# Pooled attention and an MLP on one core: value products as full-array matmuls plus 32-row tiles, batches prepared two groups ahead

## The chip, the core and the metric

The kernel runs on one core of a Trainium2 chip. A core has a matrix engine (TensorE, "PE" in the profile, with its weight loads listed apart as "PEld"), three engines for elementwise work (VectorE "DVE", ScalarE "ACT", GpSimd "POOL") and a queue engine (SyncE, "SP"), which here issues nearly all DMAs. Each engine executes its own instructions in the order in which the program emits them, and waits in place for what it needs from the others. Operands lie in SBUF, in 128 partitions; TensorE writes to PSUM, and another engine copies the result out.

The metric is device time in microseconds, the median over runs. A profiled execution of the same program gives the trace.

## What is computed

Inputs are `q`, `k`, `v` of shape 8 batches x 8 heads x 576 positions x 64, and two weight matrices. Keys and values are averaged over groups of 8 positions, so that each head has 72 pooled rows; attention is taken over these, and the result goes through an MLP without residual:

```python
k_p = k.reshape(B, H, Sp, 8, D).mean(axis=3)          # Sp = 72
v_p = v.reshape(B, H, Sp, 8, D).mean(axis=3)
attn = softmax(q @ k_p.transpose(0, 1, 3, 2) / sqrt(D))
x = (attn @ v_p).transpose(0, 2, 1, 3).reshape(B * S, H * D)   # 4608 x 512
out = gelu_tanh(x @ w_in) @ w_out                      # d_ff = 2048
```

## The kernel before

**Groups.** The 4608 tokens are worked in nine groups of 512. Group b holds the first 512 tokens of batch b; the remainder group R holds the last 64 tokens of all eight batches. The order is 0, 1, ..., 6, R, 7 (`seq`); `n_` is the place in that order. In a group, subtiles j = 0..3 have 128 tokens each.

**Stages of a group's attention.** Loads bring `q`, `k` and `v` as f32 (`load_q`, `load_main`, and `load_half` for the 64 pooled rows that do not fill a block). `cast_q` (L117) makes bf16, and `q_transpose_dma` (L198) transposes it by DMA. `pool` (L122) sums eight rows in three DVE additions into `kvb`; the factor 1/8 is applied later. `dup_k`, `k_transpose_dma` (L177) and `k_spread` (L181) give `kbd`, in which the two heads of a pair lie block-diagonally, so that one matmul yields the scores of both. `scores` (L202) and `exps` (L218) follow, then `norm` (L225): a row sum and a reciprocal on DVE, and one multiplication that writes `eb` in bf16, on DVE for subtiles 0, 2, 3 and on POOL for subtile 1. `e_transpose_dma` (L243) turns each subtile's `eb` into a part of `eT`, with pooled rows on the partitions.

**Value products.** 8 heads x 72 = 576 pooled rows lie end to end in five blocks of 128 (the first one holds 64 zeros). A head pair has 144 rows, and these lie in two blocks; `PARTS` names the two (block, operand) combinations of each pair. `spread_v` (L143) multiplies pooled v by the 0/0.125 mask `vmask` into eight operands of 128 x 128 per batch, `vbd`, on POOL. `values` (L259) runs two full products for each of the four pairs, 512 columns each, into two PSUM tiles `xo`; ACT copies each to `xT`. For group R each batch has its own 64 columns, so there are 64 products of 64 columns (L272). Group 0 uses `values_half` (L249) on halves of 256 columns.

**MLP and hooks.** `mlp` (L309) runs 64 matmuls of the hidden stage (L296, with Gelu on ACT) and then, for each of four row blocks r, 16 output matmuls (L301), a copy to `osb` and a store. Attention work of later groups is woven in by position: `at(hooks, s, f, ...)` puts a call ahead of the matmul number s. Positions 0 to 63 are the hidden stage, 64 + 16 r + fo the output stage. While group g's MLP runs, the next group n gets its scores at positions 67, 69, 78 and 82, its norms and eT transposes at 79, 82, 86 and 90, and its value products at 121, seven output matmuls before the next hidden stage. A position fixes only the order within each engine's queue; DVE, POOL and SP run ahead of PE as far as their waits allow. The stage called "group 2" in this document is the MLP of group 1 (`n_ == 1`), in which group 2's attention is made.

**What is loaded when.** Around position 91 of a group's MLP, k and v of the group after next are loaded (`load_kv`, L484); they are pooled at positions 12 to 41 of the next group's MLP. The q of the group after next is loaded at 57, cast on POOL and transposed at 91. Group R's own q is loaded in four portions at 92. Tiles `kvb` and `q_sb` have two buffers, the raw `kv` tile three (shared with the weights), `qT`, `kTd` and `eT` one.

**Group 0.** There is no MLP under which its attention could lie, so PE alternates short warm-up matmuls, transposes and scores with what DVE, ACT and POOL deliver (L361 to L463). Its MLP (`mlp_first`) works on token halves.

The softmax here doesn't subtract the row's maximum and nothing guards it: scores larger than these inputs give would overflow.

## Time and profile before

| | before |
|---|---|
| median of 3 runs | 301.4 us (301.17 to 301.49) |
| profiled execution | 301.36 us |
| its span | 299.3 us |
| PE busy | 290.7 us, 1734 matmuls |
| DVE / ACT / POOL busy | 146.7 / 158.2 / 55.5 us |
| value products, groups 1 to 7 (L266) | 56 matmuls, 512 columns |
| value products, group R (L272) | 64 matmuls, 64 columns |
| DMA moved | 56.3 MB, 188 GB/s on average |

The span runs from the first to the last instruction of the program; the profiled time has 2.1 us around it. A matmul's recorded length holds the passage through the array and overlaps its neighbours (379 ns for 512 columns); what it costs in a row of matmuls is the distance of the starts. The chain of waits shows these distances summed by piece. "Landing" is the time from a DMA's issue until its last byte is there. A line of the timeline merges neighbouring instructions of one kind: start, length, engine, line, operation, output and inputs, count, and in brackets the idle time ahead of it with what ended it.

### The profile page before, as it was taken

How to read it: one execution, taken by the hardware profiler on the slowest of the kernel's cores; microseconds unless marked ns; L12 is line 12 of the kernel's file. 1: busy time of each engine (PE TensorE's matmuls, PEld its weight loads, DVE VectorE, ACT ScalarE, POOL GpSimd, SP SyncE). 2: the span in 40 equal slices, each digit the busy share in tenths (PEclk: the TensorE clock that was granted, in tenths of full speed). 3: DMA queues.
4: the chain of work that ended last, by engine and by line, in shares of the span. 5: the costliest groups of instructions: out<-in, count | busy, mean ns of one | idle time of the engine just before them, and what ended most of it. 6: DMA issues, size and time to landing. Idle time of an engine off the chain costs nothing.

```text
span 299.3 us, 4581 instructions
## 1 busy us (share of the span) xinstructions
PE 290.7 (97%) x1734; PEld 151.6 (51%) x1734; DVE 146.7 (49%) x241; ACT 158.2 (53%) x242; POOL 55.5 (19%) x71
## 2 busy tenths in 40 slices
PE   7869999999999999999999999999999999999996
PEld 7748844445444544454445444544444544444444
DVE  6895769164706570648073807381639100920012
ACT  1477783667157715672477246724773267426500
POOL 3252033230400240024012400240024000100000
PEclk9999999999999999999999999999999999999999
DMA  7999997995699459947993599049944800351012
GB/s 235 357 387 338 384 350 132 343 279 158 135 279 250 145 127 271 269 146 126 261 297 134 119 249 301 4 107 249 276 147 101 164 36 2 79 114 37 0 70 70
DMA packets 73221, 56.32 MB, mean 188 GB/s; under 512 B 45808, under 2 KB 55408, under 8 KB 73200
## 3 DMA queue, kind: packets, MB, share of 16 engines
q1 hardware_dynamic: 73056, 55.98, 68.2%
q8 instruction: 13, 0.21, 0.3%
q10 hardware_dynamic: 144, 0.07, 0.1%
q14 instruction: 8, 0.07, 0.1%
HBM read 36.70 MB, written 9.44 MB: 154 GB/s over the span
## 4 chain that ended last, share of the span: by engine, by line
PE 91%; DMA 3%; DVE 2%; SPq 1%; POOL 1%; issue 0%; POOLq 0%
PE mm L296 41%; PE mm L301 41%; PE xo L266 4%; DMA q_sb<-in_q_dram 3%; PE sc L208 2%; PE mm L329 1%; POOL eb L231 1%; SPq L98 1%; PE xo L272 1%; PE tp L193 1%; PE sc L213 0%; DVE w_in_b L80 0%; PE tp L240 0%; DVE w_out_b L80 0%; POOL q_b L80 0%; PE xo L255 0%
## 5 line engine op out<-in xcount | busy, mean ns | idle before, releaser
L301 PE MATMUL mm<-w_out_b,gT 128*128 128x512 bf16 x560 | 128.6, 379 | 0.5 <-DVE w_out_b L80 0.5
L296 PE MATMUL mm<-xT,w_in_b 128*128 128x512 bf16 (+1 forms) x640 | 127.6, 358 | 0.5 <-DVE xT L80 0.5
L298 ACT ACTIVATE gT<-mm 128x512 bf16<-128x512 f32 (+1 forms) x160 | 88.4, 555 | 47.0 <-PE mm L296 45.9
L296 PEld LDWEIGHTS <-w_in_b 128*128 128x128 bf16 x640 | 62.2, 98 | 62.6 <-issue 0.5
L301 PEld LDWEIGHTS <-gT 128*128 128x128 bf16 x560 | 53.4, 98 | 59.7 <-DVE w_out_b L80 0.7
L80 DVE COPY osb<-mm 128x512 f32<-128x512 f32 (+2 forms) x37 | 24.3, 658 | 62.9 <-PE mm L301 60.8
L78 ACT CAST xT<-xo 128x1024 bf16<-128x1024 f32 (+1 forms) x18 | 16.6, 966 | 56.8 <-PE xo L266 49.1
L228 DVE TENSOR_REDUCE den<-e 128x8 f32<-128x576 f32 x36 | 26.5, 736 | 38.0 <-ACT e L221 37.9
L148 POOL TENSOR_TENSOR vbd<-kvb,vmask 128x256 bf16<-128x256 bf16 (+2 forms) x40 | 21.2, 553 | 113.5 <-DVE kvb L130 113.4
L128 DVE TENSOR_TENSOR kv<-kv 128x1024 f32<-128x1024 f32 (+3 forms) x20 | 22.4, 1118 | 29.7 <-DMA kv<-in_v_dram 27.7
L231 DVE TENSOR_TENSOR eb<-e,r 128x576 bf16<-128x576 f32 x28 | 27.2, 970 | 1.0
L221 ACT ACTIVATE e<-sc 128x576 f32<-128x576 f32 x36 | 22.5, 650 | 9.6 <-ACT e L221 4.0
L231 POOL TENSOR_TENSOR eb<-e,r 128x576 bf16<-128x576 f32 x8 | 10.1, 1266 | 71.5 <-ACT e L221 41.1
L80 POOL CAST q_b<-q_sb 128x2048 bf16<-128x2048 f32 (+1 forms) x7 | 15.0, 2147 | 4.1 <-DMA q_sb<-in_q_dram 4.1
L208 PEld LDWEIGHTS <-qT 128*128 128x128 bf16 x128 | 10.1, 98 | 7.0 <-ACT qT L78 0.6
L208 PE MATMUL sc<-kbd,qT 128*128 128x144 bf16 x128 | 13.2, 226 | 0.2 <-ACT qT L78 0.2
L266 PE MATMUL xo<-eT,vbd 128*128 128x512 bf16 x56 | 13.2, 379 | 0.0
L129 DVE TENSOR_TENSOR kv<-kv 128x512 f32<-128x512 f32 (+3 forms) x20 | 12.8, 640 | 0.7
L410 PE MATMUL warm<-identb 128*128 128x128 bf16 x112 | 9.1, 249 | 1.4 <-POOL vmask L398 1.4
L494 ACT ACT_TABLE_LOAD x8 | 10.3, 1283 | 0.1
L80 DVE COPY kbd<-kTd 64x288 bf16<-64x288 bf16 x12 | 5.6, 467 | 8.3 <-DMA kTd<-kvb 8.2
L314 ACT ACT_TABLE_LOAD x7 | 9.0, 1283 | 0.1
(55 smaller groups left out, 99.5 us busy)
## 6 DMA issues: line engine op xcount, KB each, us to landing
out_dram<-osb SPq DMA_DIRECT2D x31, 256.0 KB, 6.7
kv<-in_k_dram SPq DMA_DIRECT2D x7, 1024.0 KB, 6.5
q_sb<-in_q_dram SPq DMA_DIRECT2D x7, 1024.0 KB, 5.9
kv<-in_v_dram SPq DMA_DIRECT2D x7, 1024.0 KB, 9.9
w_in_s<-in_moe_w_in_dram SPq DMA_DIRECT2D x4, 1024.0 KB, 13.0
w_out_s<-in_moe_w_out_dram SPq DMA_DIRECT2D x4, 1024.0 KB, 13.8
out_dram<-osb SPq DMA_DIRECT2D x9, 128.0 KB, 2.3
kv<-in_k_dram SPq DMA_DIRECT2D x2, 512.0 KB, 3.9
```

Of the source, the lines that this page charges most:

```text
L78: eng.copy(out=out, in_=in_)
L80: eng.tensor_copy(out=out, in_=in_)
L128: add(out=t[:, :, 0:4, :], in0=t[:, :, 0:4, :], in1=t[:, :, 4:8, :], op=ALU.add)
L148: eng.tensor_tensor(out=vbd[p0:128, b, n0:n1, :].rearrange("p (c r) (hh d) -> p c (r hh) d", c=max(m, 1), d=D), in0=kvb[p0:128, 4 + c0:4 + ...
L208: nc.tensor.matmul(out=o, lhsT=qT[:, j, pr, :], rhs=kbd[:, g, pr].rearrange("d hh s -> d (hh s)"), start=True, stop=True)
L221: nc.scalar.activation(out=e.rearrange("p (x h) s -> p x (h s)", x=2), in_=sc[:, :, 0:4 * Sp], func=ACT.Exp, scale=1.0 / 64.0)
L228: nc.vector.reduce_sum(out=den, in_=e, axis=AX.X)
L231: eng.tensor_tensor(out=eb[:, j, 128 * 5 - W:].rearrange("p (h s) -> p h s", s=Sp), in0=e, in1=r.unsqueeze(2).to_broadcast([128, H, Sp]), ...
L266: nc.tensor.matmul(out=xo[:, i, :], lhsT=vbd[:, g, n, :], rhs=eT[:, :, c, :], start=(x == 0), stop=(x == 1))
L296: nc.tensor.matmul(out=hp[:, 0:c1 - c0], lhsT=w_in_b[:, ko, fo * 128:(fo + 1) * 128], rhs=st[g]["xT"][:, ko, c0:c1], start=(ko == 0), stop ...
L298: nc.scalar.activation(out=gT[:, fo, c0:c1], in_=hp[:, 0:c1 - c0], func=ACT.Gelu_apprx_tanh)
L301: nc.tensor.matmul(out=o, lhsT=gT[:, fo, r * 128:(r + 1) * 128], rhs=w_out_b[:, fo, :], start=(fo == 0), stop=(fo == FO - 1))
```

## The change

**Layout.** For each head pair, 128 of its 144 pooled v rows now form one full block; the other 16 rows of each pair go to the even partitions of 32-partition strips of a fifth block, whose odd partitions take the last 64 rows of k. `load_main` therefore steps by 144 rows for v, and `load_half` for v becomes four DMAs of 16 rows (32 KB each) instead of one of 64 rows. `eb` is written in the same arrangement, in three multiplications per subtile. The 1/8 moves from the mask to the copy out of PSUM.

**Products.** For each pair one full product of 128 rows, then one of 32 rows (a strip of `vrem` and of `eT`'s fifth block) accumulating into the same PSUM bank. The four 32-row products use four different strips of the array's rows. `values` copies one half on ACT and the other on DVE. POOL's `spread_v` makes four operands a batch instead of eight, and `rest_v` copies the rest.

**k.** The fifth transpose is full size; `k_spread` takes two small copies more for the interleaved rows.

**Order.** From `n_ == 2` on, k and v of the group after next are loaded at position 3, and pooled at 34 and 54, of the same MLP; q is loaded at 30; k is transposed at 92 and spread at 10 of the next. In `n_ == 1`, which still prepares batch 2 as before, batch 3's k and v are loaded at 24, q of group 3 stays at 57, and batch 3 is pooled at 92 and 107. In all groups the cast of q on POOL moves from 91 to 68. Group R's q moves from 92 to 110. At the start, batch 0's `load_half` goes from SP's queue to ACT's.

```diff
-
-    vbd = consts.tile([128, B, 8, 2 * D], BF16, name="vbd")
-    PARTS = {0: [(0, 0), (1, 1)], 1: [(1, 2), (2, 3)], 2: [(2, 4), (3, 5)], 3: [(3, 6), (4, 7)]}
-
-    vmask = consts.tile([128, 5, 4], BF16, name="vmask")
+    vbd = consts.tile([128, B, HP, 2, D], BF16, name="vbd")
+    vrem = consts.tile([128, B, 2, D], BF16, name="vrem")
+    vmask = consts.tile([128, 2], BF16, name="vmask")
+    vmaskf = consts.tile([128, 2], F32, name="vmaskf")
...
     def load_half(b, which, eng):
-        if which == "v":
-            eng.dma_start(out=st[b]["kv"][64:128, 4], in_=rows(v, b)[0:64])
-        else:
-            eng.dma_start(out=st[b]["kv"][0:64, 4], in_=rows(k, b)[512:576])
+        dst = st[b]["kv"][:, 4].rearrange("(m i) pl d -> i m (pl d)", i=2)
+        if which == "k":
+            eng.dma_start(out=dst[1], in_=rows(k, b)[512:576].rearrange("m pl d -> m (pl d)"))
+        else:
+            for pr in range(HP):
+                eng.dma_start(out=dst[0, 16 * pr:16 * pr + 16],
+                              in_=rows(v, b)[144 * pr + 128:144 * pr + 144].rearrange("r pl d -> r (pl d)"))
 
     def load_main(b, which, c0, c1, eng):
-        t, w0, b0 = (k, 0, 0) if which == "k" else (v, 64, 5)
-        src = rows(t, b)[w0 + 128 * c0:w0 + 128 * c1].rearrange("(c p) pl d -> p c pl d", p=128)
-        eng.dma_start(out=st[b]["kv"][:, b0 + c0:b0 + c1], in_=src)
+        t, step, b0 = (k, 128, 0) if which == "k" else (v, 144, 5)
+        src = rows(t, b).rearrange("w pl d -> w (pl d)")[0:step * 4].rearrange("(c p) e -> p c e", p=step)[0:128, c0:c1]
+        eng.dma_start(out=st[b]["kv"][:, b0 + c0:b0 + c1].rearrange("p c pl d -> p c (pl d)"), in_=src)
...
-        kvb = st[b]["kvb"]
+        o = st[b]["kvb"][:, c0:c1, 0, :]
         add = nc.vector.tensor_tensor
-        add(out=kvb[:, c0:c1, 0, :], in0=t[:, :, 0, :], in1=t[:, :, 1, :], op=ALU.add)
-
-    def pool_v_pe(b, c0, c1, eng):
+        add(out=o, in0=t[:, :, 0, :], in1=t[:, :, 1, :], op=ALU.add)
+
+    def pool_v_pe(b, c0, c1):
 
         ps = psum.tile([128, 2, D], F32, name="vp", tag="mm", bufs=4)
         for i in range(8):
             nc.tensor.matmul(out=ps, lhsT=identf, rhs=st[b]["kv"][:, c0:c1, i, :], start=(i == 0), stop=(i == 7))
-        copy(eng, st[b]["kvb"][:, c0:c1, 0, :], ps)
+        for hh in range(2):
+            nc.scalar.activation(out=vbd[:, b, c0 - 5:c1 - 5, hh, :], in_=ps, func=ACT.Copy, scale=vmaskf[:, hh:hh + 1])
...
+    def spread_v(b, p0, p1, eng):
+        eng.tensor_tensor(out=vbd[:, b, p0:p1],
+                          in0=st[b]["kvb"][:, 5 + p0:5 + p1, 0, :].unsqueeze(2).to_broadcast([128, p1 - p0, 2, D]),
+                          in1=vmask.unsqueeze(1).unsqueeze(3).to_broadcast([128, p1 - p0, 2, D]), op=ALU.mult)
+
+    def rest_v(b, eng):
+        copy(eng, vrem[:, b, 1], st[b]["kvb"][:, 4, 0, :])
...
-            pn = 64 if c == 4 else 128
-            nc.tensor.transpose(out=st[b]["kT"][:, 128 * c:128 * c + pn],
-                                in_=st[b]["kvb"][0:pn, c].rearrange("p r d -> p (r d)"), identity=identb[0:pn, 0:pn])
+            nc.tensor.transpose(out=st[b]["kT"][:, 128 * c:128 * c + 128],
+                                in_=st[b]["kvb"][:, c].rearrange("p r d -> p (r d)"), identity=identb)
...
+        kT = st[b]["kT"]
         for hh in range(2):
             p0 = 64 * hh
-            src = st[b]["kT"][p0:p0 + 64, 0:W].rearrange("d (pr hh s) -> d hh pr s", hh=2, s=Sp)[:, hh]
-            copy(engs[hh], kbd[p0:p0 + 64, b, :, hh, :], src)
+            src = kT[p0:p0 + 64, 0:W].rearrange("d (pr hh s) -> d hh pr s", hh=2, s=Sp)[:, hh, 0:4 - hh]
+            copy(engs[hh], kbd[p0:p0 + 64, b, 0:4 - hh, hh, :], src)
+
+        copy(engs[1], kbd[64:128, b, 3, 1, 0:8], kT[64:128, 504:512])
+        copy(engs[1], kbd[64:128, b, 3, 1, 8:Sp], kT[64:128, 512:640].rearrange("d (m i) -> d i m", i=2)[:, 1])
...
-        eng.tensor_tensor(out=eb[:, j, 128 * 5 - W:].rearrange("p (h s) -> p h s", s=Sp), in0=e,
-                          in1=r.unsqueeze(2).to_broadcast([128, H, Sp]), op=ALU.mult)
+        main = eb[:, j, 0:512].rearrange("p (pr w) -> p pr w", w=128)
+        rest = eb[:, j, 512:640].rearrange("p (pr w i) -> p i pr w", i=2, w=16)[:, 0]
+        eh = e.rearrange("p (pr hh) s -> p hh pr s", hh=2)
+        rh = r.rearrange("p (pr hh) -> p hh pr", hh=2)
+        for o, hh, s0, s1 in [(main[:, :, 0:Sp], 0, 0, Sp), (main[:, :, Sp:128], 1, 0, 128 - Sp), (rest, 1, 128 - Sp, Sp)]:
+            eng.tensor_tensor(out=o, in0=eh[:, hh, :, s0:s1],
+                              in1=rh[:, hh].unsqueeze(2).to_broadcast([128, HP, s1 - s0]), op=ALU.mult)
...
-    def values_half(g, half, x, eng):
-
-        xo = psum.tile([128, 2, 256], F32, name="xo", tag="mm", bufs=4)
+    def products(g, o, eT, blocks, cols):
+
+        for pr in range(HP):
+            nc.tensor.matmul(out=o[pr], lhsT=vbd[:, g, pr].rearrange("p hh d -> p (hh d)"),
+                             rhs=eT[:, blocks, pr, cols], start=True, stop=False)
+        for pr in range(HP):
+            p0 = 32 * pr
+            nc.tensor.matmul(out=o[pr], lhsT=vrem[p0:p0 + 32, g].rearrange("p hh d -> p (hh d)"),
+                             rhs=eT[p0:p0 + 32, blocks, 4, cols], start=False, stop=True)
+
+    def evict(eng, out, in_):
+
+        if eng is nc.scalar:
+            eng.mul(out, in_, 0.125)
+        else:
+            eng.tensor_scalar(out=out, in0=in_, scalar1=0.125, scalar2=None, op0=ALU.mult)
+
+    ALL = slice(0, 128)
+
+    def values_first(half, engs):
+
+        if half == 0:
+            xo = [psum.tile([128, MAIN], F32, name="xo", tag="mm", bufs=4)[:, 0:256] for _ in range(4)]
+        else:
+            xo = [t[:, i, 0:256] for t in [psum.tile([128, 2, MAIN], F32, name="xo", tag="sc", bufs=2)
+                                           for _ in range(2)] for i in range(2)]
+        products(0, xo, st[0]["eT"], slice(2 * half, 2 * half + 2), ALL)
+        for ko in range(KO):
+            evict(engs[ko], st[0]["xT"][:, ko, 256 * half:256 * half + 256], xo[ko])
+
+    def values(g, engs):
+        xo = [psum.tile([128, 2, MAIN], F32, name="xo", tag="sc", bufs=2) for _ in range(2)]
+        if g < B:
+            products(g, [xo[pr // 2][:, pr % 2] for pr in range(HP)], st[g]["eT"], slice(0, 4), ALL)
+        else:
+            for b in range(B):
+                p0 = 64 * (b % 2)
+                products(b, [xo[pr // 2][:, pr % 2, 64 * b:64 * b + 64] for pr in range(HP)], st[g]["eT"], b // 2,
+                         slice(p0, p0 + 64))
-    def values(g, half, eng):
-        xo = psum.tile([128, 2, MAIN], F32, name="xo", tag="sc", bufs=2)
...
-        copy(eng, st[g]["xT"][:, 2 * half:2 * half + 2, :], xo)
+            evict(engs[i], st[g]["xT"][:, 2 * i:2 * i + 2, :], xo[i])
...
-    load_half(0, "k", nc.sync)
-    load_half(0, "v", nc.sync)
+    load_half(0, "k", nc.scalar)
+    load_half(0, "v", nc.scalar)
...
     pool(0, 5, 7)
-    spread_v(0, nc.gpsimd, (0,))
-    pool_v_pe(0, 7, 9, nc.scalar)
-    spread_v(0, nc.gpsimd, (1,))
+    spread_v(0, 0, 2, nc.gpsimd)
+    rest_v(0, nc.gpsimd)
+    pool_v_pe(0, 7, 9)
     cast_q(0, 2, 4, nc.gpsimd)
-    spread_v(0, nc.gpsimd, (2,))
...
-    scores(0, 2)
-    exps(0, 2)
-    values_half(0, 0, 0, nc.vector)
-    scores(0, 3)
-    exps(0, 3)
-    values_half(0, 0, 1, nc.scalar)
+    for j in range(2, 4):
+        scores(0, j)
+        exps(0, j)
+    values_first(0, [nc.vector, nc.vector, nc.scalar, nc.scalar])
...
-        values_half(0, 1, 0, nc.scalar)
-        values_half(0, 1, 1, nc.vector)
+        values_first(1, [nc.scalar, nc.scalar, nc.vector, nc.vector])
...
         at(hooks, va, nc.scalar.preload_act_table_set, GELU_SET)
-        at(hooks, va, values, n, 0, nc.scalar)
-        at(hooks, va, values, n, 1, nc.scalar)
+        at(hooks, va, values, n, [nc.scalar, nc.vector])
...
+    at(hooks, 66, rest_v, 1, nc.gpsimd)
...
         at(hooks, 160, pool, 1, 5 + 2 * i, 7 + 2 * i)
-        at(hooks, 160, spread_v, 1, nc.gpsimd, (0, 1) if i == 0 else (2,))
+        at(hooks, 160, spread_v, 1, 2 * i, 2 * i + 2, nc.gpsimd)
...
     for n_, g in enumerate(seq):
         if n_ == 0:
@@ -540,21 +559,19 @@
         hooks = {}
         if n_ + 1 < len(seq):
             n = seq[n_ + 1]
-            b = B - 1 if n == R else n
-            kv = n != B - 1
             if n_ == 1:
                 at(hooks, 10, cast_q, n, 0, 4, nc.gpsimd)
                 at(hooks, 10, qT_tile, n)
                 at(hooks, 10, q_transpose_dma, n)
-            if kv:
-                t0 = 20 if n_ == 1 else 12
-                at(hooks, t0, pool, b, 0, 5)
-                at(hooks, t0, dup_k, b, 0, 5)
-                at(hooks, t0, kT_tile, b, None)
-                at(hooks, t0, k_transpose_dma, b)
-                at(hooks, t0 + 20, pool, b, 5, 9)
-                at(hooks, t0 + 21, spread_v, b, nc.gpsimd)
-                at(hooks, 56, k_spread, b, [nc.vector, nc.vector])
+                at(hooks, 20, pool, n, 0, 5)
+                at(hooks, 20, dup_k, n, 0, 5)
+                at(hooks, 20, kT_tile, n, None)
+                at(hooks, 20, k_transpose_dma, n)
+                at(hooks, 20, rest_v, n, nc.gpsimd)
+                at(hooks, 40, pool, n, 5, 9)
+                at(hooks, 40, spread_v, n, 0, 4, nc.gpsimd)
+            if n != B - 1:
+                at(hooks, 56 if n_ == 1 else 10, k_spread, kv_of(n), [nc.vector, nc.vector])
             for j in range(4):
...
         if n_ + 2 < len(seq):
             n2 = seq[n_ + 2]
             if n2 != R:
-                at(hooks, 57, q_tile, n2)
-                at(hooks, 57, load_q, n2, 0, 4, nc.sync)
-            at(hooks, 91, cast_q, n2, 0, 4, nc.gpsimd)
+                at(hooks, 57 if n_ == 1 else 30, q_tile, n2)
+                at(hooks, 57 if n_ == 1 else 30, load_q, n2, 0, 4, nc.sync)
+            at(hooks, 68, cast_q, n2, 0, 4, nc.gpsimd)
             at(hooks, 91, qT_tile, n2)
             at(hooks, 91, q_transpose_dma, n2)
-            at(hooks, 91, load_kv, n2)
+            if n2 != B - 1:
+                b = kv_of(n2)
+                at(hooks, 24 if n_ == 1 else 3, load_kv, b)
+                t0, t1 = (92, 107) if n_ == 1 else (34, 54)
+                at(hooks, t0, pool, b, 0, 5)
+                at(hooks, t0, dup_k, b, 0, 5)
+                at(hooks, t0, rest_v, b, nc.gpsimd)
+                at(hooks, t1, pool, b, 5, 9)
+                at(hooks, t1, spread_v, b, 0, 4, nc.gpsimd)
+                at(hooks, 107 if n_ == 1 else 92, kT_tile, b, None)
+                at(hooks, 107 if n_ == 1 else 92, k_transpose_dma, b)
         if n_ == 1:
-            at(hooks, 92, q_tile, R)
+            at(hooks, 110, q_tile, R)
         if 1 <= n_ <= 4:
-            at(hooks, 92, load_q, R, n_ - 1, n_, nc.sync)
+            at(hooks, 110, load_q, R, n_ - 1, n_, nc.sync)
         mlp(g, hooks, n_ + 1 == len(seq))
```

## The prediction

> **What bounds the kernel now.** I read the page first (busy shares, the 40 slices, the chain by line), then the chain in order of time, then single stages in the timeline. The profiled execution took 301.36 us, a span of 299.3 and 2.1 around it, against a median of 301.4 for the runs shown, so its own durations can be summed.
>
> ```profile
> span 299.3 us, 4581 instructions
> PE 290.7 (97%) x1734; PEld 151.6 (51%) x1734; DVE 146.7 (49%) x241; ACT 158.2 (53%) x242; POOL 55.5 (19%) x71
> PE 91%; DMA 3%; DVE 2%; SPq 1%; POOL 1%; issue 0%; POOLq 0%
> ```
>
> TensorE is the bound: from about 23 us to the end the chain is PE alone. What leaves PE shortens the kernel, and what makes PE wait lengthens it. In the chain by time (start, length, what), these pieces price the products:
>
> ```profile
> 32.85 0.35 PE kT L174 x5
> 33.20 0.98 PE mm L296 x8
> ...
> 82.22 1.73 PE xo L266 x8
> ...
> 220.69 0.65 PE mm L301 x3
> 221.33 0.37 PE sc L213 x8
> 221.71 0.54 PE mm L301 x2
> ...
> 234.90 1.87 PE xo L272 x64
> ```
>
> Eight value products take 1.73, so 0.216 each. L213 works on half the columns of the array: eight of them take 0.37 where four full ones (L208) take 0.25, and the two L301 behind them 0.54 instead of 0.43. So two half-width products run together, and entering and leaving that mode costs 0.11 to 0.12 each. L174 has a fifth transpose of 64 rows: 0.35 instead of five times 0.055, and the eight behind it 0.98 instead of 0.87. A row mode pays the same, near 0.1 in and 0.1 out.
>
> The second reading is group 2, the first stage whose neighbours are moved (timeline: start, length, engine, line):
>
> ```profile
> 58.48 7.20 SPq L199 DMA_TRANSPOSE qT<-q_b  x1
> 65.77 1.22 SPq L178 DMA_TRANSPOSE kTd<-kvb  x1
> 67.04 0.58 SPq L110 DMA_DIRECT2D q_sb<-in_q_dram  x1
> 72.64 0.76 DVE L231 TENSOR_TENSOR eb<-e,r 128x576 bf16<-128x576 f32 x1
> 75.03 1.15 POOL L231 TENSOR_TENSOR eb<-e,r 128x576 bf16<-128x576 f32 x1 [7.64 <-ACT e L221]
> 76.12 2.42 POOL L80 CAST q_b<-q_sb 128x2048 bf16<-128x2048 f32 x1
> 76.20 4.17 SPq L244 DMA_TRANSPOSE eT<-eb  x3
> 77.79 1.36 DVE L231 TENSOR_TENSOR eb<-e,r 128x576 bf16<-128x576 f32 x1
> 80.32 0.69 DVE L80 COPY osb<-mm 128x512 f32<-128x512 f32 x1 [0.56 <-PE mm L301]
> 82.06 1.89 PE L266 MATMUL xo<-eT,vbd 128*128 128x512 bf16 x8
> ```
>
> See how little room there is: the last eT transpose is issued at 79.18 and lands 2.6 later (that tile's view), at 81.75; the products start at 82.06. POOL works in order: its norm first, then the cast of the next q.
>
> **The parts, with their sum.**
>
> *Products, groups 1 to 7 (seven times).* Four full products 0.864, 0.1 in, four 32-row products, 0.1 out. No row shows four 32-row tiles. If they run together like L213's pairs, they cost one product, 0.216; if one by one, 0.864. I take together (nearest row L213): 1.28 instead of 1.73, -0.45 each, -3.15. Bounds: -4.5 (no switch cost) to +1.35 (one by one).
> The Trainium skill, "TensorE: Matmul & The Clock Gate", Part 3, has four 32-row tiles of 512 columns at 3.07 times the speed, not four; by it they take 0.28 and the seven groups gain 0.4 less. No run here shows it yet.
>
> *Products of the remainder group.* 64 products at 0.029 were 1.87. Now eight batches, each 4 x 0.029, a switch pair of 0.2 and 0.03 to 0.06: about 0.35, 2.8 in all, +0.9. Bounds: -0.7 without switch cost, +1.5 one by one.
>
> *Group 0 and the k transposes.* Its second half goes from eight of 0.109 to 0.74: -0.13; its first half is paced by DVE, so nothing. The 64-row transpose becomes a full one: -0.17. PE in all: **-2.55** (bounds -5.4 and +2.9).
>
> *Norms.* One eb operation becomes three (288, 224, 64 elements). f32 operations here fit 0.157 + 1.044 per thousand elements (1280: 1.49; 640: 0.83; 576: 0.76), so three are 1.07, less 0.16 if they overlap as independent ones do (two osb copies take 1.28): +0.15 to +0.43 on DVE. POOL: 1.15 + 2 x 0.145 = 1.44 (0.145 from vbd rows 0.40 and 0.655). Against that, the cast moved ahead no longer slows the last eb (1.36 here, 0.76 in group 7 with no cast after it). Last eb between +0.05 and +0.9 later; room 0.3: PE waits 0 to 0.6 in groups 3 to 6, up to 0.75 in group 7. I take 0.25 for four and 0.1 for the last: **+1.0**.
> In group 1 four norms on DVE delay the pooling of v by 0.6 to 1.7; POOL then spreads pairs 2 and 3 (0.655) before their product: 0 to 1.1, **+0.3**.
>
> *Head.* SP loses two issues (1.2), but those loads wait for bandwidth (14.65 is where the last q lands), so I cost that at nothing. ACT issues five loads (0.59 each) ahead of its table load, idle until 9.59 anyway; then three k spread copies instead of one, +0.45 before qT and e. DVE's norms 0 and 1 end about 0.65 later, two evictions of 256 instead of one of 512 +0.2, POOL's norm 2 (2.09 on the chain) +0.3. Bounds 0.2 and 1.7; **+1.1**.
>
> *Other moves.* Evictions go to ACT and DVE side by side; 1.5 of L301 hides them while DVE is free. k_spread gets two small copies, at hook 10 under the hidden stage. POOL's spreading falls from 2.7 to 1.2 a batch, and copies of the rest (under 0.4) fit its idle time. Pooling at 34 and 54 lies under 13.8 of L296. In groups from 3 on, loads go out after the last store, about 117 to 122 in the stage that began at 85; at some 270 to 330 GB/s q lands near 130 and the cast ends near 133, 2 before the norm on POOL: hidden. Without that cover the case below repeats.
>
> *Group 2.* Here the moved steps collide. SP issues in order: transposes until 66.99, then batch 3's seven loads (k, k rest, four of v rest, v, about 0.55 each; three more issues than before) until 71, and only then q of group 3, issued before at 67.04. Its data go behind 2.36 MB. Batch 2's k and v (same sizes) took from q's landing at 55.19 to 61.95, 6.8. So q lands between 71.3 + 5.6 = 76.9 (5.6 is its own issue to landing) and about 78.7; before 72.6. Its cast now stands before POOL's norm of subtile 1: norm done 2.42 + 1.44 later, 80.8 to 82.6. On SP the transposes of subtiles 1, 2, 3 stand behind it: 2 x 1.3 + 2.6, so eT is there at 86.0 to 87.8 and PE waits 4.0 to 5.7. **+5.0**.
> Then the clock: after the last matmul, at 296.35, it still reads 1.00, and from 298.90 on 0.50:
>
> ```profile
> 1.43 4.45 PE L410 MATMUL warm<-identb 128*128 128x128 bf16 x44 [1.43 <-POOL vmask L398]
> 6.08 1.39 PE L410 MATMUL warm<-identb 128*128 128x128 bf16 x22
> ...
> 298.90:299.28 0.38, 0.00 (x0) 0.00 (x0) 0.00 (x0) 0.00 (x0) 0.00 (x0) 0.50 0.00 0
> ```
>
> 2.5 idle is enough. From cold, 44 warm-ups take 4.45 where 44 at the later pace take 2.78: **+1.7** (0 if it does not fall, 2.0 at most).
> Against the four small v loads stands a rule of the Trainium skill, "DMA: Bandwidth & Descriptors", Rules for kernel authors: under 64 KB a transfer is mostly overhead. These are 32 KB. The page's table has 0.95 us for 64 KB; if three extra transfers each cost that in sequence, q would land an estimated 2.9 later and not 1.8, and the sum rise by 1.1. The rows here price an issue at 0.5 to 0.6 whether it is 128 or 1024 KB, and the sum goes by them.
>
> Sum: -2.55 + 1.0 + 0.3 + 1.1 + 5.0 + 1.7 = +6.55, **307.9 us**.
>
> **Rivals.** *B, DVE sets group 2.* If q came in time, DVE still has batch 3's pooling at hooks 92 and 107 in front of its eviction: from 79.15, 3.07 + 0.68 + 2.53 + 0.69 + 1.2 = 87.3, while the hidden stage wants that half of xT at about 85.3. Wait 2.0 (0.4 with every operation uncontended), below what drops the clock. It is covered in the main case, as DVE is done while PE waits. Sum 301.36 - 2.55 + 1.0 + 0.3 + 1.1 + 2.0 = 303.2. For it: DMA share is only 0.62 between 67 and 74. Against: SP's order.
>
> *C, the four tiles run one by one.* PE +2.9 instead of -2.55: 313.3. Against it L213's pairs.
>
> *D, faster.* One thing decides: q of group 3 lands by 72.6, as before, because SP's 7.20 on the first q transpose is gone or batch 3's loads run beside it. POOL is then on time, the clock holds; with DVE's wait at 0.4 and the norms hidden: 301.36 - 2.55 + 1.1 + 0.3 + 0.4 = 300.6, down to 299.7 if the head costs 0.2. Against it: seven issues alone take until 71.
>
> **How the numbers follow.** A 0.67 (own range 305.0 to 310.5), B 0.14, C 0.04, D 0.12, about no change 0.03. 0.2%, 0.6 us, is about what this kernel's measurement can tell from no change; D's near edge gives a little to it. Slower 0.84, same 0.04, faster 0.12. The range 302.0 to 310.8 takes in A but its top, and B; D, C and A's top are left out, under 2 in 10.
>
> **What would show it.** Right: in group 2 the POOL cast of q starts near 78 and ahead of eb; the products wait 4 to 6 on eT; matmuls behind them run at half clock; q's loads land after v's. Products: four full at 0.216, a gap near 0.1, four starts within some 10 ns, a gap near 0.1; the remainder's about 2.8. Wrong: PE without a gap at group 2, the four tiles 0.2 apart, or waits of several us in every group.

## The result, and the profile after

The changed kernel takes **321.98 us** (median of 4 runs, 320.97 to 323.26) against 301.29 for the kernel before on the same chip: 1.0688 times as long, interval 1.0649 to 1.0727. The forecast was slower at 307.9, range 302.0 to 310.8: the direction held, the size did not. The profiled execution took 321.95 us, with a span of 320.2 against 299.3; the 20.9 us between the spans are what has to be placed.

The head of the page after: span, busy times, and the shares of the chain of waits by engine.

```profile
span 320.2 us, 4630 instructions
PE 291.4 (91%) x1708; PEld 148.6 (46%) x1734; DVE 162.7 (51%) x321; ACT 151.2 (47%) x239; POOL 46.6 (15%) x65
PE 57%; DVE 22%; DMA 10%; SPq 4%; issue 3%; ACT 1%; POOL 1%; ACTq 1%; DVEq 0%; POOLq 0%
```

PE is busy for as long as before, yet its share of the chain fell from 91% to 57%: PE did not get more work, it waits. The chain of before was PE alone from 23 us on; now DVE holds 22% of it and DMA 10%.

Where it waits is read from the starts of the value products. The timeline of after, PE alone, one line per group (start, length, line, operation, count, and in brackets the idle time ahead of it with what ended it):

```profile
53.99 1.03 PE L254 MATMUL xo<-eT,vbd 128*128 128x512 bf16 x4
91.01 1.86 PE L254 MATMUL xo<-eT,vbd 128*128 128x512 bf16 x4 [7.28 <-issue]
123.87 1.02 PE L254 MATMUL xo<-eT,vbd 128*128 128x512 bf16 x4
157.62 1.49 PE L254 MATMUL xo<-eT,vbd 128*128 128x512 bf16 x4 [3.67 <-issue]
190.94 1.02 PE L254 MATMUL xo<-eT,vbd 128*128 128x512 bf16 x4 [1.65 <-DMA eT<-eb]
224.05 1.02 PE L254 MATMUL xo<-eT,vbd 128*128 128x512 bf16 x4 [3.02 <-DMA eT<-eb]
...
286.60 1.02 PE L254 MATMUL xo<-eT,vbd 128*128 128x512 bf16 x4
```

Groups 2, 4, 5 and 6 wait 7.28, 3.67, 1.65 and 3.02, together 15.6. Groups 1, 3 and 7 do not. In two of the lines the four products also take 1.86 and 1.49 instead of 1.02: the clock. Three stretches of group 2 (length, busy time of PE, PEld, DVE, ACT and POOL, then the granted clock, DMA share and GB/s):

```profile
83.90:90.90 7.00, 0.00 (x0) 0.00 (x0) 4.80 (x8) 0.00 (x0) 2.85 (x5) 0.68 0.39 75
91.00:96.30 5.30, 5.29 (x15) 1.55 (x16) 1.23 (x1) 1.02 (x1) 0.00 (x0) 0.50 0.96 200
96.70:101.00 4.30, 4.30 (x22) 1.94 (x21) 1.09 (x5) 2.39 (x4) 0.00 (x0) 1.00 0.79 244
```

After the long wait PE works some 5.3 us at 0.50, which costs half of that, 2.65. Behind the wait of group 4 the same view gives 0.61 over 4.38 us, 1.7 lost.

The balance of the spans: waits +15.6, clock +4.3, the start +2.05 (first output matmul at 40.75 instead of 38.70), products -3.1, group R +1.1. That is +19.95 of the 20.9; about 0.95 is not placed.

Group 2 in the timeline of after:

```profile
72.37 0.51 SPq L115 DMA_DIRECT2D q_sb<-in_q_dram  x1
...
81.10 2.21 POOL L82 CAST q_b<-q_sb 128x2048 bf16<-128x2048 f32 x1 [13.55 <-DMA q_sb<-in_q_dram]
81.59 2.39 DVE L134 TENSOR_TENSOR kv<-kv 128x640 f32<-128x640 f32 x1
83.27 2.27 POOL L233 TENSOR_TENSOR eb<-e,r 128x288 bf16<-128x288 f32 x3
...
85.56 3.84 SPq L246 DMA_TRANSPOSE eT<-eb  x3
```

This is the collision that the prediction described. The q of group 3 is issued behind batch 3's loads at 72.37 and lands 8.6 later; POOL waits 13.55 for it with subtile 1's norm queued behind; that norm ends at 85.54, and SP issues three eT transposes in a row at 85.56.

Group 4, where the prediction saw nothing, in the same view:

```profile
139.83 1.49 DVE L133 TENSOR_TENSOR kv<-kv 128x1280 f32<-128x1280 f32 x1 [10.17 <-DMA kv<-in_v_dram]
...
142.92 1.22 DVE L133 TENSOR_TENSOR kv<-kv 128x1024 f32<-128x1024 f32 x1
142.93 1.19 ACT L218 ACTIVATE e<-sc 128x576 f32<-128x576 f32 x2
...
145.24 0.74 DVE L225 TENSOR_REDUCE den<-e 128x8 f32<-128x576 f32 x1
...
146.26 2.64 DVE L233 TENSOR_TENSOR eb<-e,r 128x288 bf16<-128x288 f32 x3
...
146.39 2.12 POOL L82 CAST q_b<-q_sb 128x2048 bf16<-128x2048 f32 x1
```

DVE stands idle for 10.17 until the first part of the batch is there, and then pools until 145.3, although the exponentials of the first subtile were written by about 143.6. Then the first `eb` takes 2.64 where three multiplications take 0.90 elsewhere; POOL casts q within that time, from 146.39 to 148.51. Group 6 shows the same, with pooling until 211.9 and 2.64 for the first `eb`; in group 5 the pooling ends in time, and the first `eb` takes 2.05, again beside the cast.

### The profile page after: what moved, and what is told of

Its sections match the earlier page's. It is cut to its first block, busy times and chain, and to the rows that moved or that the text cites. A ratio compares the mean times of both kernels' runs of the same rounds, so it can differ in the third digit from the quotient of the medians.

```text
span 320.2 us, 4630 instructions
## 1 busy us (share of the span) xinstructions
PE 291.4 (91%) x1708; PEld 148.6 (46%) x1734; DVE 162.7 (51%) x321; ACT 151.2 (47%) x239; POOL 46.6 (15%) x65
## 4 chain that ended last, share of the span: by engine, by line
PE 57%; DVE 22%; DMA 10%; SPq 4%; issue 3%; ACT 1%; POOL 1%; ACTq 1%; DVEq 0%; POOLq 0%
PE mm L313 29%; PE mm L318 20%; DVE eb L233 6%; DMA kv<-in_v_dram 5%; DVE den L225 5%; DMA eT<-eb 3%; PE xo L254 3%; DVE kv L133 3%; DVE kv L134 2%; SPq L97 2%; DVE osb L82 2%; DVE r L227 2%; DMA kTd<-kvb 1%; PE xo L258 1%; PE mm L346 1%
## 5 line engine op out<-in xcount | busy, mean ns | idle before, releaser
L264 ACT ACTIVATE xT<-xo 128x1024 bf16<-128x1024 f32 (+1 forms) x12 | 9.5, 809 | 79.6 <-PE xo L258 79.6
L233 DVE TENSOR_TENSOR eb<-e,r 128x288 bf16<-128x288 f32 (+2 forms) x84 | 34.8, 468 | 1.0
L254 PE MATMUL xo<-eT,vbd 128*128 128x64 bf16 (+2 forms) x68 | 12.0, 302 | 15.9 <-issue 10.9
L266 DVE TENSOR_SCALAR xT<-xo 128x1024 bf16<-128x1024 f32 (+1 forms) x12 | 11.3, 956 | 26.5 <-PE xo L258 26.5
L233 POOL TENSOR_TENSOR eb<-e,r 128x288 bf16<-128x288 f32 (+2 forms) x24 | 14.9, 646 | 56.9 <-DVE r L227 47.5
L82 POOL CAST q_b<-q_sb 128x2048 bf16<-128x2048 f32 (+1 forms) x7 | 12.9, 1846 | 32.9 <-DMA q_sb<-in_q_dram 32.9
L82 POOL COPY vrem<-kvb 128x64 bf16<-128x64 bf16 x8 | 2.2, 272 | 102.4 <-DVE kvb L135 102.4
L254 PEld LDWEIGHTS <-vbd 128*128 128x128 bf16 x68 | 4.7, 99 | 21.6 <-issue 19.3
L134 DVE TENSOR_TENSOR kv<-kv 128x512 f32<-128x512 f32 (+3 forms) x20 | 14.4, 718 | 0.7
L150 POOL TENSOR_TENSOR vbd<-kvb,vmask 128x512 bf16<-128x512 bf16 (+1 forms) x9 | 8.4, 939 | 37.1 <-DVE kvb L135 37.1
```

The lines of the kernel that those rows point to most:

```text
L82: eng.tensor_copy(out=out, in_=in_)
L134: add(out=t[:, :, 0:2, :], in0=t[:, :, 0:2, :], in1=t[:, :, 2:4, :], op=ALU.add)
L233: eng.tensor_tensor(out=o, in0=eh[:, hh, :, s0:s1], in1=rh[:, hh].unsqueeze(2).to_broadcast([128, HP, s1 - s0]), op=ALU.mult)
L254: nc.tensor.matmul(out=o[pr], lhsT=vbd[:, g, pr].rearrange("p hh d -> p (hh d)"), rhs=eT[:, blocks, pr, cols], start=True, stop=False)
L266: eng.tensor_scalar(out=out, in0=in_, scalar1=0.125, scalar2=None, op0=ALU.mult)
```

## The experiments

Each was timed against the kernel before on the same chip. The letters in the expectations: O, the moved steps make the waits; L, the layout does; O1 and O2 split O into the cast ahead of POOL's norm and the pooling on DVE. K, T and S are explained where they come up. "Waits" below are the idle times ahead of the value products, as in the table of lines above.

**Layout alone, order alone.** The changed kernel with every position of the kernel before, and the kernel before with the changed positions.

```diff
# e1_layout_only: the changed kernel with
-                at(hooks, 24 if n_ == 1 else 3, load_kv, b)
-                t0, t1 = (92, 107) if n_ == 1 else (34, 54)
+                at(hooks, 91, load_kv, kv_of(n2))
-            at(hooks, 68, cast_q, n2, 0, 4, nc.gpsimd)
+            at(hooks, 91, cast_q, n2, 0, 4, nc.gpsimd)
...
# e2_order_only: the same in the other direction, on the kernel before
```

> The changed kernel with the order of before: k and v of the group after next loaded at 91 and pooled at 12 and 32 of the next MLP, q cast at 91, group R's q at 92. Layout, products, norms and loads stay as changed. Theory O (the moved steps make the waits ahead of the value products: 7.7, 0.5, 4.1, 2.0, 3.4 and 0.4 us in the trace of the changed kernel, 16.8 beyond the usual 0.2 each, and some 4 us at half clock): 300 to 304 us, products about 1.28 us a group, no wait over 1 us ahead of them. Theory L (the layout makes them: three multiplications per norm and four small v loads delay eT and the data): still above 312 us.

> The kernel before with only the order of the change: loads at 24 or 3, pooling at 92 and 107 or 34 and 54 of the same MLP, q cast at 68, group R's q at 110; layout, products and the single multiplication per norm stay as before. Theory O: 314 to 322 us, with waits of 2 to 8 us ahead of the value products of groups 2, 4, 5 and 6. Theory L: 300 to 304 us.

Layout alone: 308.89, ratio 1.0251 (1.0236 to 1.0266). Order alone: 321.68, ratio 1.0669 (1.0626 to 1.0711), with waits of 6.75, 3.00, 0.93 and 3.02 and the clock at 0.50 for 5.3 us behind the first. So the order by itself makes a loss as large as that of the changed kernel, but the layout is not free either: it lies between the 304 that O allowed at most and the 312 that L asked for, and both expectations of the first run fell. The two costs, 7.6 and 20.4, do not add up to the 20.7 of both together. Both make PE wait at the same place, ahead of the value products, and group 3 shows one reason more: it waits 1.31 with the layout alone (below) and not at all in the changed kernel, where the cast stands at 68.

Most of the layout's 7.6 is five waits, of 1.42, 1.31, 1.68, 1.30 and 1.38 in groups 2 to 6, 7.1 together; the later start (+1.7), group R and the shorter products nearly cancel. The timeline of layout alone, group 2:

```profile
73.82 0.90 DVE L233 TENSOR_TENSOR eb<-e,r 128x288 bf16<-128x288 f32 x3
...
76.35 1.66 POOL L233 TENSOR_TENSOR eb<-e,r 128x288 bf16<-128x288 f32 x3 [8.68 <-ACT e L218]
...
77.11 2.98 DVE L233 TENSOR_TENSOR eb<-e,r 128x288 bf16<-128x288 f32 x3
77.95 2.05 POOL L82 CAST q_b<-q_sb 128x2048 bf16<-128x2048 f32 x1
78.04 5.18 SPq L246 DMA_TRANSPOSE eT<-eb  x3
...
84.83 1.02 PE L254 MATMUL xo<-eT,vbd 128*128 128x512 bf16 x4 [1.42 <-DMA eT<-eb]
```

Subtile 0's three multiplications take 0.90; subtile 2's, which begin before POOL's cast, take 2.98 and end at 80.09, just behind the cast's end at 80.00. This is taken up again below (theory K).

**Which of the moved steps.** The cast put back to 91, the pooling put back behind the norms, and both; the early loads stay in all three.

```diff
# e3_cast_at_91
-            at(hooks, 68, cast_q, n2, 0, 4, nc.gpsimd)
+            at(hooks, 91, cast_q, n2, 0, 4, nc.gpsimd)
# e4_pool_late
-                t0, t1 = (92, 107) if n_ == 1 else (34, 54)
+                t0, t1 = 92, 122
...
-                at(hooks, 107 if n_ == 1 else 92, k_transpose_dma, b)
+                at(hooks, 107, k_transpose_dma, b)
# e5_cast_and_pool_late: both
```

> The changed kernel with one placement undone: the cast of q on POOL goes back from 68 to 91, behind POOL's norm. Theory O1 (the cast in front of POOL's norm is most of it, as predicted): group 2's wait ahead of the products falls below 1.5 us, the others too, total 303 to 308 us. Theory O2 (most of it is DVE's pooling in front of norms and eviction): group 2 keeps 2 to 4 us, now behind the products on the eviction, groups 4 to 6 keep 2 to 4 us each, total 312 to 318 us. Theory L: unchanged, 320 to 323 us.

> The changed kernel with the pooling moved behind the norms: blocks 0 to 4 at 92, blocks 5 to 8 at 122 behind the value products, k transposed at 107, in all groups; the cast stays at 68. Theory O2: groups 4 to 6 lose nearly all of their wait, group 2 keeps the 5 us that POOL's order costs, total 306 to 311 us. Theory O1: only little falls away, 316 to 321 us, as POOL still waits for q's landing in each group. Theory L: unchanged.

> The changed kernel with both placements moved: the cast of q back at 91 and the pooling behind the norms, at 92 and 122; loads stay at 24 and 3. Theory O (the order's waits are these two placements together): the 4 to 8 us waits go, and what stays is what the layout alone showed with the old order, 1.5 us ahead of the products in each of groups 2 to 6: 307 to 311 us. Rival (the late loads themselves, issued behind the stores, set a wait of their own): above 313 us.

The cast at 91: 315.52, ratio 1.0484 (1.0462 to 1.0505). The wait of group 2 falls from 7.28 to 1.03, but groups 4 to 6 keep 2.29, 2.47 and 1.28, and group 3, which had none, now waits 1.32. The total lies where O2 put it, though two of its waits are shorter than O2's 2 to 4. In group 2 a second wait comes up, the one that the prediction's rival B priced at 2.0 (timeline):

```profile
88.89 1.22 DVE L266 TENSOR_SCALAR xT<-xo 128x1024 bf16<-128x1024 f32 x1
...
90.16 3.18 PE L313 MATMUL mm<-xT,w_in_b 128*128 128x512 bf16 x14 [1.79 <-DVE xT L266]
```

DVE's half of `xT` stands behind the pooling of batch 3, and the hidden stage waits 1.79 for it.

The pooling late: 313.76, ratio 1.0422 (1.0399 to 1.0445): less than O1 expected, more than O2. Group 2 waits 7.32 as in the changed kernel. The waits of groups 5 and 6 are gone, and group 4 keeps 2.02, now for POOL's copy of the rest of batch 5's v, which ends at 154.28; the products start at 154.30. So neither O1 nor O2 is most of it alone.

Both: 308.69, ratio 1.0247 (1.0232 to 1.0262), with waits of 1.10, 1.31, 1.65, 1.30 and 1.26. That is layout alone (308.89) within its interval. So undoing the two placements takes away all that the order adds, 13.3 us of the changed kernel's time; with them undone, the early loads, the later group R loads and `k_spread` cost nothing measurable in the total. How much of the 13.3 is the placement and how much that the loads now go out only one stage ahead isn't separated: no run has the new placements with the old loads. And the five waits are not all those of layout alone: in group 2 of this run the cast (from 81.58) comes after all multiplications, and the 1.10 there is taken up with the last run.

**What the layout's waits are.** K: a DVE multiplication with both inputs in SBUF stands still while a POOL instruction reads SBUF, and three short ones leave the cast two openings to get in between. T: three multiplications are slow by themselves. The first run of this pair moves the cast of layout alone to ACT; the second leaves it on POOL but writes `eb` in one multiplication, as before, and so leaves out the new column arrangement of `eb`.

```diff
# e6_cast_on_act: layout alone with
-            at(hooks, 91, cast_q, n2, 0, 4, nc.gpsimd)
+            at(hooks, 91, cast_q, n2, 0, 4, nc.scalar)
# e7_one_multiplication: layout alone with
-        for o, hh, s0, s1 in [...]:
-            eng.tensor_tensor(out=o, in0=eh[:, hh, :, s0:s1], ...)
+        eng.tensor_tensor(out=eb[:, j, 128 * 5 - W:].rearrange("p (h s) -> p h s", s=Sp), in0=e,
+                          in1=r.unsqueeze(2).to_broadcast([128, H, Sp]), op=ALU.mult)
```

> The layout with the old order, and the cast of q at 91 moved from POOL to ACT. Theory K (a multiplication on DVE that meets a POOL instruction reading SBUF stands still until POOL is through; three multiplications instead of one let the 2 us cast in between, so that subtile 2's take 2.98 us instead of 0.90): the waits of 1.5 us ahead of groups 2 to 6 fall to 0.2 to 0.5, subtile 2's three take 1.3, total 300.5 to 302.5 us. Theory T (three short multiplications and their order are slower by themselves): waits stay above 1 us, total above 306 us.

> The layout with the old order and the cast on POOL at 91, but each norm writes eb by one multiplication in the arrangement of before. This leaves out the new arrangement of the columns, so the products take their rows from the wrong places; sizes and instructions of everything else are the same. Theory K and theory T both expect the waits to fall to about 0.2 us: 299.5 to 301.5 us. If they stay above 1 us, the norms are not their cause.

Cast on ACT: 302.31, ratio 1.0029 (1.0017 to 1.0040). The waits are gone, and the same three multiplications, beside the same three on POOL, take 1.29 (timeline of that kernel):

```profile
77.08 1.66 POOL L233 TENSOR_TENSOR eb<-e,r 128x288 bf16<-128x288 f32 x3 [8.54 <-ACT e L218]
...
77.83 1.29 DVE L233 TENSOR_TENSOR eb<-e,r 128x288 bf16<-128x288 f32 x3
```

One multiplication with the cast on POOL: 301.18, ratio 1.0000 (0.9990 to 1.0009). T falls with the first. The second, which both theories expected, shows that the three multiplications carry the waits; K stands with both. The groups by form show which piece carried the loss (shape, count, busy time, mean ns of one); first layout alone, then the cast on ACT:

```profile
L233 DVE TENSOR_TENSOR eb<-e,r 128x64 bf16<-128x64 f32 x28 | 18.2, 648 | 0.0
```

```profile
L233 DVE TENSOR_TENSOR eb<-e,r 128x64 bf16<-128x64 f32 x28 | 8.0, 284 | 0.0
```

The smallest of the three, 64 elements, is the slowest: 28 of them cost 10.2 us more, about 2 for each of the five groups that wait. It is the one that finds the cast running: in group 2 of layout alone the three stand at 77.11 to 77.85, 77.78 to 78.25 and 78.18 to 80.09, and POOL's cast at 77.95 to 80.00.

The same lines lay open in the profile of before: POOL's cast ran from 76.12 to 78.54, and DVE's single multiplication, begun at 77.79, ended 0.61 behind it; POOL's norm ended at 76.18 and DVE's multiplication begun at 75.78 again ended 0.61 behind. The Trainium skill, "SBUF — State Buffer", section "SBUF: two separate sides", says that a DVE operation with two SBUF inputs and a GpSimd operation that reads SBUF share an exclusive lock, and that whichever starts first keeps it for its whole instruction. The runs agree: with three instructions in place of one, DVE gives the lock up twice, and 0.90 becomes 2.98.

**What is left of the layout, and a version that beats both.** With the cast on ACT, group R's eight alternations of 128-row and 32-row products and the start are left. First all full products of group R ahead of all 32-row ones (one change of mode), and subtile 2's norm of group 0 on DVE; then that norm back on POOL; then the loads of the rest of k and v at the start in two more arrangements. S: the small loads of v on ACT's queue hold up group 0.

```diff
# e8_strips_last: cast on ACT with
...
-            for b in range(B):
-                products(b, ...)
+            for part in (full, strips):
+                for b in range(B):
+                    part(b, ..., b == (0 if part is full else B - 1))
...
-    norm(0, 2, nc.gpsimd)
+    norm(0, 2, nc.vector)
# e9a_strips_norm_pool: that with
-    norm(0, 2, nc.vector)
+    norm(0, 2, nc.gpsimd)
# e9b_v_rest_first: that with
-    load_half(0, "k", nc.scalar)
+    load_half(0, "k", nc.sync)
# e9c_v_rest_on_sp: that and
-    load_half(0, "v", nc.scalar)
+    load_half(0, "v", nc.sync)
```

> The layout with the old order and the cast on ACT, and two things more: in group R all 32 full products come first and all 32 strip products behind them, so that the array changes its mode once and not eight times (2.9 us to about 1.4), and group 0's norm of subtile 2 is made on DVE and not on POOL (its first multiplications there take 2.5 us, on DVE 0.9). 1.5 to 2.5 us below the kernel with the cast on ACT alone: 298.0 to 300.5 us. If a change of mode costs nothing, group R gains nothing.

> The layout with the old order, the cast on ACT and group R's strips last; group 0's norm of subtile 2 is back on POOL, since on DVE it held up the cast of w_in that PE waits for next (2.7 us gap). Group R's change of order alone: 1.4 us less than with the cast on ACT alone (302.3), so 300.4 to 301.5 us. If the change of mode were not what the strips cost, nothing is gained.

> The same, and at the start the k rest goes back to SP's queue while the four small v loads stay on ACT's. In the trace they land one by one at 6.57, 8.28, 8.95 and 9.49 us, and the pooling of the block that holds the k rest waits for the last. Theory S (small loads on the second queue take turns with SP's large ones, and the last of them sets group 0): they land one turn earlier, 0.3 to 0.8 us less in total. Rival (group 0 is set by DVE's longer norms and evictions): no difference.

> The same, and all five loads of the rests at the start are on SP, ahead of q. Theory S: the v rest lands near 7.2 us instead of 9.5, the first hidden matmul comes 1.5 to 2.2 us earlier, total 298.5 to 300.0 us, below the kernel before. Rival (DVE's work sets group 0, or the three issues more delay q's first half by as much): 300.4 us or more.

The strips last with the norm on DVE: 301.34, ratio 1.0013 (0.9988 to 1.0038), above the 298.0 to 300.5 expected. The norm on DVE stood ahead of a share of the cast of `w_in`, and the hidden stage of group 0 then waited 2.52 for that cast. The cast itself took 2.92, from 22.78, where DVE's others of this size take about 1.2: POOL's share of the same cast had begun at 22.72 and ran until 24.62. With the norm on POOL: 300.75, ratio 0.9975 (0.9958 to 0.9991). Group R in the chain of that kernel (start, length, what):

```profile
234.65 0.93 PE xo L253 x32
235.58 0.34 PE xo L259 x32
```

1.27 instead of the 2.8 of the changed kernel, and a third less than the 1.87 of before.

The loads of v first on ACT's queue: 300.80, ratio 0.9967 (0.9943 to 0.9991), no different; the last of them landed at 8.11 instead of 8.53, and the first hidden matmul stayed at 20.0. All five on SP's queue, behind the two of k: **299.69, ratio 0.9944 (0.9923 to 0.9965)**. They landed by 7.0 and the first hidden matmul started at 19.38, a gain of 0.6 where 1.5 to 2.2 was expected. In the chain of this kernel group 0 hangs on the second half of q, issued at 6.76 and landed at 15.02, as in the kernel before (4.84 and 14.65); with the norm back on POOL it had landed at 12.9. So S holds in its direction, for the place of the loads and not for their order on ACT, and the rival holds in part: with five loads put ahead of it on SP, q lands later, though its second half and not its first. By its median this is the fastest kernel of the study, 0.6% below the one before; that it beats the two others of this series is less sure, as its four runs (299.57 to 300.10) lie within the ten of the kernel with v first on ACT (298.74 to 301.68).

**The order again, with the cause removed.** The changed kernel with the pooling behind the norms and the cast at 91 on ACT.

```diff
# e10_order_cast_act
-            at(hooks, 68, cast_q, n2, 0, 4, nc.gpsimd)
+            at(hooks, 91, cast_q, n2, 0, 4, nc.scalar)
-                t0, t1 = (92, 107) if n_ == 1 else (34, 54)
+                t0, t1 = 92, 122
...
-                at(hooks, 107 if n_ == 1 else 92, k_transpose_dma, b)
+                at(hooks, 107, k_transpose_dma, b)
```

> The changed kernel in the new order with the pooling at 92 and 122 and the cast of q at 91 on ACT: loads at 24 and 3, two groups ahead. Theory K and O together (late pooling, and a POOL cast that stops DVE, are all that the new order costs): 301.5 to 303.0 us, as with the old order and the cast on ACT. Rival (the later loads have a price of their own): above 304 us.

302.57, ratio 1.0040 (1.0028 to 1.0053), against 302.31 for the old order with the same cast. One wait is left, 1.10 in group 2, as long as with both placements undone and the cast on POOL, so it isn't the cast's. There the four eT transposes take 3.1 to 6.7 from issue to landing, against 2.6 with the old order, while batch 3's loads and q's are under way; that the loads delay them is a reading and not tested. In the total, loading two groups ahead is neither a loss nor a gain here.

## Why the prediction was right or wrong

**Products, -0.45 each: right.** The chain of the one-multiplication kernel has, for group 5, the four full products and the four 32-row ones:

```profile
174.24 0.86 PE xo L249 x4
175.11 0.33 PE xo L253 x4
```

The sum is 1.19, and with the 0.1 on leaving, 1.28 from the first of them to the next output matmul (group 3 of after: 123.87 to 125.15). The four tiles run together; 0.33 with the entry is what the prediction's 0.1 and 0.216 give. Rival C is out. Group R was given +0.9, 2.8 in all; in the chain of after its products run from 255.04 to 257.84, 2.8, with 0.16 more until the next matmul: +0.9 to +1.1 against 1.87.

**Head, +1.1: undersized, +2.05.** The step that was too small is "ACT issues five loads (0.59 each) ahead of its table load, idle until 9.59 anyway". I looked at what the issues cost ACT and not at when the data land. The chain after, at the start:

```profile
2.74 0.61 ACTq L97
3.35 0.03 issue
3.38 5.85 DMA kv<-in_v_dram
...
9.36 0.44 DVE kv L133
```

The last load of v takes 5.85, and the pooling of the block starts at 9.36 instead of 7.43. The first hidden matmul starts at 20.73 instead of 19.26, 1.47 of the 2.05. The new layout with these loads on ACT starts its output stage at 40.2 to 41.3 (layout alone, cast on ACT, one multiplication, norm back on POOL, one profile of each), with all on SP at 39.03, against 38.70 before.

Not all of this is the loads. The output stage waits last for a cast of `w_out` on DVE, beside another one on POOL (timeline, first after, then all loads on SP):

```profile
37.72 1.89 POOL L82 CAST w_out_b<-w_out_s 128x2048 bf16<-128x2048 f32 x1 [4.35 <-DMA w_out_s<-in_moe_w_out_dram]
39.05 1.64 DVE L82 CAST w_out_b<-w_out_s 128x2048 bf16<-128x2048 f32 x1
```

```profile
37.76 1.22 DVE L82 CAST w_out_b<-w_out_s 128x2048 bf16<-128x2048 f32 x1
38.24 2.48 POOL L82 CAST w_out_b<-w_out_s 128x2048 bf16<-128x2048 f32 x1 [4.99 <-DMA w_out_s<-in_moe_w_out_dram]
```

The one that begins first keeps its short time: DVE's takes 1.22 in the kernel before and with all loads on SP, and 1.55 to 2.64 in the profiles where POOL's is under way (2.59 with one multiplication, 1.79 with the norm back on POOL). No run changed this cast alone.

**Norms, +1.0: the mechanism was missed.** Uncontended, three multiplications take 0.90 against 0.76, +0.14, at the near end of the "+0.15 to +0.43". But the prediction took "slows the last eb (1.36 here, 0.76 in group 7 ...)" for a slowdown that a cast brings with it. The runs show an order of turns, and three instructions lose more turns than one. With the cast at 68 subtile 2 is indeed spared (1.29 in groups 3, 4 and 6), but in groups 4 to 6 the cast meets the first `eb` instead. In the order of before this costs 1.3 to 1.7 in each of five groups, 6.6 us, while I had 0.25 and 0.1.

**Group 2, +5.0 and the clock +1.7: mechanism right, both too small.** The cast came at 81.10 (near 78 by my working) ahead of `eb`, and PE waited for eT, 7.28 in place of 4.0 to 5.7. Three terms: q was issued at 72.37 and landed at 80.95, 2.3 beyond my late bound, of which some 1.8 is the later start of everything; POOL's three multiplications took 2.27 and not 1.44, beside DVE's pooling, whose second addition itself took 2.39 in place of 0.83 beside the cast; and the half clock lasted some 5.3 us, a loss of 2.65, beyond the 2.0 that I called the most, a bound that no row gave. "2.5 idle is enough" held for some waits and not for others (last section).

**"In groups from 3 on ... hidden, 2 before the norm": the step that failed.** It is the largest miss: waits of 3.67, 1.65 and 3.02 and a second half-clock stretch of 1.7, 10 us together, which my sum put at nothing. The "85" of that step doesn't fit its 117 to 122: the hidden stage that starts next in the trace of before starts at 115.6, and counted from there the loads go out 1.5 to 6.5 after the start and q lands 14.4 after it.

In group 3 the step held. Its loads left SP 1.4 to 6.1 after the start of the hidden stage (96.31), q landed 14.4 after it, POOL's cast ended at 114.14 and its norm began at 116.75, without a wait of PE. In group 4 the loads left SP between 129.78 and 135.36, behind the last two stores, which SP issued at 128.67. That is 3.1 to 8.7 after the start of the hidden stage (126.67); v landed at 142.07 and q at 144.88, 15.4 and 18.2 after it, whereas the scores of group 4 stand at 14.5. Position 3 in the program does not time SP. The cover was 2 us wide, and all that was hidden under it, DVE's pooling and POOL's cast, came out at once: DVE pooled until 145.3 while the first exponentials lay ready, and the cast then held up the first `eb` until 148.9. The prediction's own sentence, "Without that cover the case below repeats", has the outcome, a wait in the later groups, which I priced at nothing; it doesn't have the path. In group 2 POOL's norm stands behind the cast; in groups 4 and 6 DVE's first norm stands behind the pooling, and in groups 4 to 6 its multiplications are then stopped by the cast.

**Rivals.** B's wait on DVE's eviction exists, 1.79 for the 2.0 given, once the cast is out of the way. D, faster: its condition, q in time, is met in group 2 by no kernel with the new positions, so no run shows what it would have taken; the nearest that spares the norms is the old order with the cast on ACT, 302.31. The 0.84 on slower held by the predicted path, group 2 (7.28, and 2.65 for the clock); the other waits only made it more. The range ended at 310.8 because it had one group wait where four did.

## What to carry to other kernels

A position in an order written out by hand times only PE; for the other engines it says what stands behind what, so for every step moved forward, ask what it will wait for and what is queued behind it, and check by the landing times that its cover is wider than the error of the estimate. Before an elementwise operation on DVE is split into pieces, look at what POOL runs beside it: each boundary is a place where a long POOL instruction can get in, and the piece behind it pays for the whole of that. And where mode changes on PE cost 0.2 a pair, as here, gather what needs the mode: in group R, going in and out of it once and not eight times gave 1.5 us back.

## What was not expected of the hardware

- DVE and POOL block each other in whole instructions: 0.90 became 2.98 on DVE, and in the other direction POOL's three went from 1.66 to 2.27 when they met DVE's pooling. A cast on DVE shows the same: 1.22 when it began first, 2.64 when POOL's cast of 1.90 began 0.34 ahead of it (v first on ACT).
- Four loads of 32 KB on ACT's queue, issued from 1.4 to 4.0 us beside the large loads of SP, landed last at 8.5 in the kernel with the norm back on POOL; on SP's own queue, issued from 2.5 to 5.0, they landed by 7.0. The medians of the two kernels differ by 1.1 us, of which the first hidden matmul shows 0.6.
- 32 products of 32 rows and 64 columns take 0.34 us, 0.011 each, in four row tiles, where 32 full products of 64 columns take 0.93.
- The granted clock fell to 0.50 in an idle stretch of 7.3 us and stayed there for some 5.3 us of work, and after 3.67 us its mean was 0.61 over 4.4 us. The length of the wait alone doesn't decide: with the cast at 91, a wait of 2.47 in group 5 also brought it to 0.61 over the next 4.26 us, while the changed kernel's wait of 3.02 in group 6 left it at 1.00.
